# Another order for the seven products of a fused attention and MoE kernel, and for all its steps

## The chip, the cores and the metric

One core of a Trainium2 chip runs the whole program. The metric is the device time of one execution in microseconds (us); lower is better. The core has five engines with a queue each: TensorE (PE in the profile; PEld is its weight load), VectorE (DVE), ScalarE (ACT), GpSimd (POOL) and SyncE (SP), which here only issues DMA transfers.

## The reference, cut to what matters

Attention for 4 batches, 8 heads, 768 positions, 64 channels: each query sees the keys within 16 positions of it, and for each block of 32 positions one summary (the largest key channel by channel, the mean value):

```python
scores_l = scale * np.matmul(q, k.transpose(0, 1, 3, 2))      # masked to |i - j| < 16
scores_s = scale * np.einsum('bhsd,bhnd->bhsn', q, k_sum) + np.log(block)
a = softmax(np.concatenate([scores_l, scores_s], axis=-1))
x = np.matmul(a, np.concatenate([v, v_sum], axis=2))          # to 3072 rows of 512
h = x @ w_in                                                  # 512 -> 2048
return (h - np.tanh(h)) @ w_out                               # 2048 -> 512
```

## The kernel before, in words

The 3072 rows are eight units u of 384 rows (three tiles of 128). For each unit, attention runs in two halves of four heads (`block`): 48 small score products, row minimum (DVE), exponential (ACT), normalization, transposes ("p turn"), 12 value products into a bank, and a copy to SBUF. The MoE runs over 16 slices f of 128 columns of w_in: a first product into a PSUM bank of tag "pH" (two of them), an elementwise chain, a split of its result into a high and a low float32r part ("g high", "g low"), and a second product ("out", three tasks of three matmuls of 512 columns) into the banks pY0 to pY2.

A float32 product is made of three float32r products, so each matrix is kept as a high and a low part. The 32 weight slices are loaded as raw words and converted on DVE, ACT and POOL (`convert`), one after the other through the first 140 us.

From unit 2 on two units are paired, and the first product is a product of 2 by 2 blocks made of seven products instead of eight (`moe_in_seven`, L994): B11, B21, T2, T1, T3, T4 and B22, six matmuls of 384 columns each. Their left operands are slices of w_in and sums of them that `make_sums` wrote to a DRAM tensor (scr) around 80 to 235 us; `load_sums` reads them back in four loads t = 0 to 3 for each of the eight g of a pair (products 0 and 1 need t = 0, products 2 and 3 t = 1, 4 and 5 t = 2, product 6 t = 3). These loads take turns in three buffers of the tag "wraw", so the load t = 1 of the next g may start when this g's products 4 and 5 are done. Each g has two banks, z and y. Products 0, 2, 4 and 6 add up in z, 1, 3 and 5 in y (3 starts y anew); a "part" copies z to SBUF (ACT or DVE) and a "join" adds a stored part to y (DVE).

The order of the work is written out. The kernel first lists 3628 tasks with what each reads and writes; `ORDER` is a permutation of their numbers, and each engine gets its tasks in that order. `ON` has a letter for each task: which engine takes it where several could. `FILL` names tasks of PE ahead of which so many idle matmuls (two records of 128 columns each) are put, to keep PE at work through a wait. `Plan.follow` (L148) walks the list. A task waits by semaphore for what it reads and for the buffer that it writes; an engine's queue is in order, so a task that waits holds up all behind it. A helper records every instruction, so all of them carry line 56 in the profile, and are told apart by tiles.

The tile names needed here: raw weights land in wraw, their converted form in tmp and then wf; the q, k, v of the first batch land in wg, gt, gu, gv and vw; qT, kT, oo are transposed q and k; prob, probT and stat belong to the softmax; the loads of vw for a half of a unit ("v load" of 16 to 80 rows of 1 KB, 11 for each half of a unit) and three "mean put" must all have landed before the value products.

Of the kernel before, what the change touches and what calls it, by code (L numbers as in the profile page):

```python
# [21 lines left out]
RAWB = 3  # L22
# [61 lines left out]
class Plan:  # L89
# [20 lines left out]
    def add(self, kind, costs, go, r=(), w=()):  # L110
# [15 lines left out]
        for base in dict.fromkeys(key[0] for key in (*r, *w)):  # L126
# [15 lines left out]
            self.touch.setdefault(base, []).append(t)  # L142
        t.after.discard(t)
        t.order.discard(t)
        t.order -= t.after
        return t

    def follow(self, idle):  # L148

        tasks = [self.tasks[n] for n in ORDER]  # L150
        free = dict.fromkeys((PE, DVE, ACT, POOL, SP), 0.65)
        dma, held, left = 0.0, {DVE: 0.0, POOL: 0.0}, 0.0
        clock, used, seen, done = Clock(), {}, {}, []
        spot, rest, lanes = 0, self.fill, [0.0] * 8
        for t in tasks:
            e = next(iter(t.costs)) if len(t.costs) == 1 else {"D": DVE, "A": ACT, "P": POOL, "S": SP}[ON[t.index]]
            assert all(a in seen for a in (*t.after, *t.order)), t.name
            t.engine, t.cost = e, t.costs[e]
            now = max([free[e]] + [seen[a] for a in t.after] + [at for b in t.banks for a, at in used.get(b, {}).items() if a != e])
            if e == PE:  # L160
                cost, go = idle
                if now > free[PE]:
                    free[PE] = max(free[PE], min(now, seen.get(self.tasks[0], now)))
                if spot == 1:
                    free[PE] = max([free[PE]] + [min(now, at) for a, at in used.get(rest[3], {}).items() if a != PE])
                for _ in range(FILL.get(t.index, 0) if FILL is not None else int(0.7 * (now - free[PE]) / cost) if spot < 2 and now - free[PE] > 0.4 else 0):
# [171 lines left out]
def program(  # L338
# [652 lines left out]
    def gu(u, f):  # L991
        return (lambda: at(("gu", u, f))), [(("gu", u, f), 0)]
# [348 lines left out]
```

## Time and profile before

| | |
|---|---|
| time, median of 3 runs | 660.22 us (660.14 to 660.5) |
| the profiled execution: its time | 663.1 us |
| its span, first to last instruction | 661.4 us |
| mean granted TensorE clock | 0.995 |
| PE / PEld / DVE / ACT / POOL busy | 632.8 / 532.5 / 447.7 / 453.3 / 151.2 us |
| HBM read and written | 88.87 and 20.97 MB |

The page has the busy time of each engine, the span in 40 slices, the DMA queues, the chain of work that ended last, and groups of instructions. Further views give the same for a stretch of the span, the idle time of an engine by what ended it (waits), and the instructions in order of time (timeline). Matmuls overlap in the pipeline, so a row's duration is longer than the step from one matmul to the next.

### The profile page before, as it was taken

What the parts mean: (1) busy time and instruction counts of PE and PEld (TensorE: products, weight loads), DVE (VectorE), ACT (ScalarE), POOL (GpSimd) and SP (SyncE); (2) the same over time, 40 slices, a digit from 0 to 9 for tenths busy, and PEclk for the clock granted to TensorE, in tenths of its full rate; (3) what the DMA queues carried; (4) which work ended last, traced back from release to release, by engine and by line L of the source; (5) the groups of instructions that cost most, each with busy time, mean ns of one, the idle gap of its engine ahead of it and who ended that gap; (6) DMA issues with size and microseconds to landing.
All of it is one profiled execution on the core that took longest, in us unless ns stands there. A gap on an engine that the chain in (4) does not pass through costs nothing.

```text
span 661.4 us, 15115 instructions
## 1 busy us (share of the span) xinstructions
PE 632.8 (96%) x5297; PEld 532.5 (81%) x5297; DVE 447.7 (68%) x1285; ACT 453.3 (69%) x1371; POOL 151.2 (23%) x240
## 2 busy tenths in 40 slices
PE   5779989999899999999999999999999999999997
PEld 4746557778779888989888789989888799999885
DVE  2778999996998884655778874455766944334472
ACT  3578899989798863545689873644789853433773
POOL 2002310103301410113524421313343211112101
PEclk9899999999999999999999999999999999999999
DMA  7678887746687686667453465655443155444001
GB/s 201 158 212 241 230 238 223 240 146 188 209 282 259 210 266 174 194 211 219 135 156 82 115 184 178 207 163 175 136 130 84 59 173 191 146 166 153 33 17 66
DMA packets 120736, 113.24 MB, mean 171 GB/s; under 512 B 45008, under 2 KB 88528, under 8 KB 120656
## 3 DMA queue, kind: packets, MB, share of 16 engines
q1 hardware_dynamic: 117216, 109.19, 54.3%
q10 hardware_dynamic: 3440, 3.05, 1.4%
q8 instruction: 43, 0.70, 0.5%
q14 instruction: 37, 0.30, 0.2%
HBM read 88.87 MB, written 20.97 MB: 166 GB/s over the span
## 4 chain that ended last, share of the span: by engine, by line
PE 72%; DMA 12%; DVE 6%; ACT 4%; SPq 3%; issue 2%; DVEq 0%; ACTq 0%
PE pY L56 34%; PE pH L56 31%; PE pS L56 4%; DMA wraw<-in_moe_w_in_dram 3%; PE pX L56 3%; DMA raw<-in_k_dram 3%; SPq L56 3%; ACT prob L56 2%; DMA raw<-in_q_dram 1%; DMA scr<-wraw 1%; DMA wraw<-in_moe_w_out_dram 1%; DVE tmp L56 1%; DVE prob L56 1%; DVE kT L56 1%; DVE wraw L56 1%
## 5 line engine op out<-in xcount | busy, mean ns | idle before, releaser
L56 ACT ACTIVATE prob<-prob,stat 128x120 f32<-128x120 f32 x294 | 107.8, 386 | 35.4 <-DVE stat L56 34.8
L56 PE MATMUL pY<-wl,gh 128*128 128x512 f32 x288 | 113.4, 394 | 0.2 <-DVE wl L56 0.2
L56 PE MATMUL pH<-wf,wraw 128*128 128x384 f32 x552 | 112.1, 338 | 1.3 <-ACT gu L56 1.2
L56 PEld LDWEIGHTS pH<-wf,wraw 128*128 128x128 f32 x552 | 97.4, 188 | 7.1 <-ACT gu L56 1.6
L56 PE MATMUL pH<-wg,wraw 128*128 128x384 f32 x432 | 84.0, 337 | 0.2
L56 PE MATMUL pY<-wh,gh 128*128 128x512 f32 x204 | 83.2, 408 | 0.0
L56 PE MATMUL pY<-wh,gl 128*128 128x512 f32 x204 | 80.7, 396 | 0.0
L56 PEld LDWEIGHTS pH<-wg,wraw 128*128 128x128 f32 x432 | 75.9, 188 | 3.8 <-DMA wraw<-scr 0.5
L56 PE MATMUL pY<-wg,gh 128*128 128x512 f32 x168 | 68.6, 408 | 0.0
L56 ACT ACTIVATE gu<-gu 128x384 f32<-128x384 f32 x128 | 65.8, 520 | 1.9
L56 PE MATMUL pY<-wg,gl 128*128 128x512 f32 x168 | 66.5, 396 | 0.4 <-DVE gl L56 0.4
L56 PE MATMUL pH<-o,wf 128*128 128x384 f32 x188 | 65.5, 445 | 0.0
L56 POOL TENSOR_TENSOR gl<-gu,gh 128x384 fp32r<-128x384 f32 x28 | 29.5, 1055 | 144.3 <-ACT gh L56 64.1
L56 PEld LDWEIGHTS pY<-wl,gh 128*128 128x128 f32 x288 | 54.2, 188 | 9.1 <-DVE wl L56 0.6
L56 ACT ACTIVATE gv<-pH 128x384 f32<-128x384 f32 x37 | 18.1, 489 | 45.3 <-PE pH L56 45.1
L56 PEld LDWEIGHTS pH<-o,wf 128*128 128x128 f32 x188 | 34.9, 191 | 14.8 <-issue 0.9
L56 PEld LDWEIGHTS pY<-wh,gl 128*128 128x128 f32 x204 | 38.2, 187 | 8.9 <-DVE gl L56 0.4
L56 PE MATMUL pY<-wf,gh 128*128 128x512 f32 x108 | 44.5, 439 | 0.0
L56 PEld LDWEIGHTS pY<-wh,gh 128*128 128x128 f32 x204 | 38.3, 188 | 7.0 <-issue 0.5
L56 POOL TENSOR_TENSOR gu<-gu,gt 128x384 f32<-128x384 f32 x25 | 25.7, 1030 | 79.8 <-ACT gu L56 69.9
L56 ACT ACTIVATE gt<-gu 128x384 f32<-128x384 f32 x48 | 24.9, 519 | 26.9 <-DVE gu L56 25.9
L56 POOL TENSOR_TENSOR prob<-prob,stat 128x120 f32<-128x120 f32 x45 | 18.5, 415 | 89.3 <-DVE stat L56 80.3
(210 smaller groups left out, 1382.5 us busy)
## 6 DMA issues: line engine op xcount, KB each, us to landing
wraw<-scr SPq DMA_DIRECT2D x72, 512.0 KB
wraw<-in_moe_w_in_dram SPq DMA_DIRECT2D x16, 512.0 KB
wraw<-in_moe_w_out_dram SPq DMA_DIRECT2D x16, 512.0 KB
scr<-wraw SPq DMA_DIRECT2D x16, 512.0 KB
wraw<-scr SPq DMA_DIRECT2D x24, 256.0 KB
raw<-in_q_dram SPq DMA_DIRECT2D x54, 96.0 KB
vw<-in_v_dram SPq DMA_DIRECT2D x60, 80.0 KB
raw<-in_k_dram SPq DMA_DIRECT2D x48, 96.0 KB
```

The costliest lines, as they stand in the source:

```text
L56: return lambda *args, **kwargs: self._tc.keep_in_program_order(op(*args, **kwargs))
```

## The change

Four things are edited; the computation stays as it was.

1. `moe_in_seven`: the products run in the order B11, B21, T2, T1, T3, B22, T4. The part s3 is now taken from y after T1, the join c22 from z after T3, the join c12 from y after B22, and the part c21 from z comes last. In the last pair of units, the odd g use the banks pX and pS1 in place of two of tag pH.
2. The transfers "v load" of batch 0 and "mean put" of units 0 and 1 may go to POOL's DMA queue; `ON` sends ten there (v loads 8, 13, 20, 23, 26, 38, 40; mean puts 0, 2, 5). Before, SP issued all of them.
3. `ORDER`, `ON` and `FILL` are new throughout.
4. Buffers wl, vw, qT and kT are taken from another pool; a DRAM tensor scr2 and functions for a second seven-product scheme are added (`make_out_sums`, `moe_out_seven`), which nothing calls, since `OUT7` is empty.

```diff
-FILL = {125: 18, 154: 12, 158: 2, 190: 14, 188: 6, 286: 2}
+FILL = {125: 16, 154: 12, 158: 2, 190: 10, 188: 1, 215: 2, 262: 2, 286: 2}
+OUT7 = ()
-    def dma(kind, go, nbytes, run, r=(), w=(), both=False):
+    def dma(kind, go, nbytes, run, r=(), w=(), both=False, any_queue=False):
...
+        elif small_only and any_queue:
+            t = plan.add(kind, {SP: cost, POOL: cost}, go, r, w)
...
-        z, y = bank(("z", u, g), "pH"), bank(("yx", u, g), "pH")
+        tags = ("pX", "pS1") if u == NU - 2 and g % 2 else ("pH", "pH")
+        z, y = (bank((n, u, g), tag) for n, tag in zip(("z", "yx"), tags))
...
         product(0, "B11", z, True)
         product(1, "B21", y, True)
-        part(lambda: at(s1), [(s1, 0)])
-        join(c11, k11, s1)
+        part(z, lambda: at(s1), [(s1, 0)])
+        join(y, c11, k11, s1)
         product(2, "T2", z, False)
-        part(lambda: at(s2), [(s2, 0)])
+        part(z, lambda: at(s2), [(s2, 0)])
         product(3, "T1", y, True)
+        part(y, lambda: at(s3), [(s3, 0)])
         product(4, "T3", z, False)
-        part(lambda: at(s3), [(s3, 0)])
-        join(c22, k22, s3)
+        join(z, c22, k22, s3)
+        product(5, "B22", y, False)
+        join(y, c12, k12, s2)
         load_sums(u, g, 3)
         product(6, "T4", z, False)
-        part(c21, k21)
-        product(5, "B22", y, False)
-        join(c12, k12, s2)
+        part(z, c21, k21)
```

What the new lists say, with tasks of the two lists matched by name:

| KB of transfers issued, up to and with | before | after |
|---|---|---|
| weight load 0 | 3696 | 3632 |
| k loads 8 to 11 (second half of heads) | 4400 | 4080 |
| weight load 1 | 5296 | 5152 |
| all of vw for unit 0, heads 0 to 3 | 5792 | 5792 |
| all of vw for unit 0, heads 4 to 7 | 8000 | 7488 |
| weight load 3 | 7152 | 7376 |
| weight load 4 | 7808 | 8336 |
| q loads 8 to 11 (unit 1) | 8464 | 8480 |
| weight load 9 | 11584 | 11712 |

On PE the first 160 us hold the same tasks at places that differ by a few. On DVE the transpose of k loads 8 to 11 now stands ahead of the last step of weight 0 and of the next six minima, that of k loads 12 to 15 behind four of these; one normalization that stood ahead of them, the scaling of weights 2 and 3, and the means 5 and 6 of the first value sums went to ACT. On POOL, mean put 2 and six further transfers stand behind two normalizations of the first softmax. Ahead of the score products of unit 3, heads 4 to 7 (the seventh block), the copy "top put 3" went from ACT to DVE, and the first product of unit 1, slice 5, which stood directly ahead of them, is now followed by a value and an out task. The 16 guards of softmax sums moved from DVE to POOL are spread over the whole run. Products of PE between the products 4 and 5 of a g, whichever comes last, and product 2 of the next g: before 4.0 to 7.1 us at the durations of the trace, in 15 of 21 cases under 4.3; after 4.5 to 9.3. The tail behind the last product is as before, but for the queue of two stores.

## Rows read from the trace of the kernel before

**Rows 1.** Windows by stage: length, busy time of each engine (instructions), PE clock, DMA share, GB/s
```profile
0.00:16.50 16.50, 8.77 (x122) 8.11 (x125) 4.66 (x5) 5.20 (x20) 4.43 (x28) 1.00 0.76 201
16.50:33.00 16.50, 12.52 (x274) 11.54 (x266) 11.53 (x43) 8.83 (x36) 0.63 (x2) 0.90 0.63 159
...
100.00:150.00 50.00, 50.00 (x491) 36.31 (x486) 48.69 (x134) 46.38 (x135) 4.57 (x5) 1.00 0.69 203
...
550.00:600.00 50.00, 50.00 (x265) 46.66 (x264) 20.24 (x39) 19.58 (x49) 4.15 (x5) 1.00 0.47 159
```

**Rows 2.** Waits of PE over the span: total us, times, longest
```profile
PE pH L56 <- DMA gt<-in_v_dram: 6.7, 2, 4.0
PE pS L56 <- DVE prob L56: 4.6, 2, 4.0
PE pY L56 <- ACT tmp L56: 3.2, 1, 3.2
PE pH L56 <- ACT gt L56: 2.7, 1, 2.7
...
PE pH L56 <- ACT gu L56: 1.2, 1, 1.2
```

**Rows 3.** Timeline of PE, 18 to 50 us: start, length, what, [idle before]
```profile
18.34 2.94 PE L56 MATMUL pY<-ident 128*128 128x128 f32 x24
25.27 0.89 PE L56 MATMUL pS<-ident,prob 128*120 128x128 f32 x4 [3.98 <-DVE prob L56]
...
27.11 4.54 PE L56 MATMUL pY<-ident 128*128 128x128 f32 x28
...
35.51 0.45 PE L56 MATMUL pS<-probT,vw 120*64 120x64 f32 x8 [0.33 <-DMA vw<-in_v_dram]
...
46.02 0.95 PE L56 MATMUL pY<-probT,wg 120*64 120x64 f32 x24 [3.21 <-ACT tmp L56]
```

**Rows 4.** Timeline of DVE, 20 to 33 us
```profile
22.97 0.43 DVE L56 TENSOR_SCALAR tmp<-wraw 128x512 f32<-128x512 f32 x1 [2.26 <-DMA wraw<-in_moe_w_in_dram]
...
25.13 0.88 DVE L56 SCALAR_TENSOR_TENSOR wf<-wraw,tmp 128x512 uint32<-128x512 uint32 x1
25.93 0.27 DVE L56 CUSTOM_DVE_ANT_0 prob<-pX,mask 128x120 f32<-128x120 f32 x1
...
27.67 1.83 DVE L56 STREAM_TRANSPOSE wg<-wg 128x768 f32<-128x768 f32 x2
```

**Rows 5.** Timeline of SP's DMA issues, 0 to 60 us
```profile
16.71 1.00 SPq L56 DMA_DIRECT2D vw<-mean  x1
17.77 0.47 SPq L56 DMA_DIRECT2D wraw<-in_moe_w_in_dram  x1
...
26.86 6.06 SPq L56 DMA_DIRECT2D vw<-in_v_dram  x5
```

**Rows 6.** Waits of SP's queue, 0 to 60 us
```profile
SPq L56 <- DMA raw<-in_q_dram: 3.8, 1, 3.8
```

**Rows 7.** Windows of 4 us, columns as in Rows 1
```profile
16.00:20.00 4.00, 3.98 (x154) 3.73 (x155) 2.01 (x8) 0.48 (x2) 0.00 (x0) 1.00 0.42 105
...
32.00:36.00 4.00, 3.67 (x121) 2.79 (x117) 3.53 (x18) 3.67 (x14) 0.25 (x1) 1.00 0.51 142
...
48.00:52.00 4.00, 4.00 (x33) 2.35 (x32) 2.72 (x6) 1.94 (x5) 0.00 (x0) 0.72 0.93 267
```

**Rows 8.** Timeline of POOL, 10 to 60 us
```profile
25.08 0.39 POOL L56 TENSOR_TENSOR prob<-prob,stat 128x120 f32<-128x120 f32 x1 [10.16 <-DVE stat L56]
```

**Rows 9.** Timeline of ACT, 163 to 172 us
```profile
167.59 0.53 ACT L56 ACTIVATE kT<-kT 128x384 f32<-128x384 f32 x1 [2.46 <-DVE kT L56]
```

**Rows 10.** Timeline of SP's DMA issues, 232 to 262 us
```profile
253.91 4.29 SPq L56 DMA_DIRECT2D wraw<-scr  x3
```

**Rows 11.** Timeline of PE, 258 to 260 us
```profile
259.73 0.59 PE L56 MATMUL pH<-wf,wraw 128*128 128x384 f32 x2 [1.19 <-ACT gu L56]
```

**Rows 12.** Chain that ended last, pieces in order of time: start, length
```profile
227.85 4.28 DMA wraw<-scr
```

**Rows 13.** Timeline of PE, 540 to 552 us
```profile
548.10 2.25 PE L56 MATMUL pH<-wg,wraw 128*128 128x384 f32 x12
```

More of the change, by code (lines that the diff above doesn't have):

```diff
@@ L177, in follow @@
                 now = max(now, free[PE])
-                if t.kind in ("in", "out", "p turn"):
+                if t.kind in ("in", "out", "out half", "p turn"):
                     t.cost, left = t.cost + max(left, 0.0), -1.0
@@ L181, in follow @@
                     t.cost, left = t.cost + (self.ENTERS if left < 0 else 0.0), self.LEAVES.get(t.kind, 0.0)
+            elif SP in t.costs and e == POOL:
+                now = max(now, others.pop(0), held[DVE])
+                t.issue, t.ahead, held[POOL] = 0.62, 1.8, now + 0.62
             elif SP in t.costs:
@@ L672, in program @@
         made[SCR] = spool.tile([FH, 8, P, 2 * DH], F32, name="scr")
+        made[SCR2] = spool.tile([5, FH, P, 2 * DH], F32, name="scr2")
     def make_sums(g):
@@ L1017, in product, with part, join @@
             do("in", PE, 1.055, go, r=[(st, 0)] + [key for c in range(2) for _, key in x_of[x, u, c]], w=[(ps, 0)])
-        def part(out, keys):
-            either("part", {ACT: 0.4, DVE: 0.49}, lambda e: copy(e, out(), at(z)[:, :U]), r=[(z, 0)], w=keys)
-        def join(out, keys, x):
-            do("join", DVE, 0.47, lambda: vector.tensor_tensor(out(), at(y)[:, :U], at(x), op=ALU.add), r=[(y, 0), (x, 0)], w=keys)
+        def part(ps, out, keys):
+            either("part", {ACT: 0.4, DVE: 0.49}, lambda e: copy(e, out(), at(ps)[:, :U]), r=[(ps, 0)], w=keys)
+        def join(ps, out, keys, x):
+            do("join", DVE, 0.47, lambda: vector.tensor_tensor(out(), at(ps)[:, :U], at(x), op=ALU.add), r=[(ps, 0), (x, 0)], w=keys)
         for t in range(3):
@@ L1274, in program @@
                 convert(2 * m2[1] + 1)
-            moe_out(*m2)
-            if m2[1] == order_of(m2[0])[-1]:
+            if not seven_out(m2[0]):
+                moe_out(*m2)
+            if not seven_out(m2[0]) and m2[1] == order_of(m2[0])[-1]:
                 for i in range(NT):
@@ L1289, in program @@
                 moe_in_seven(*m)
-            moe_act(*m)
+                if seven_out(m[0]):
+                    for n in range(4):
+                        moe_act(m[0] + n % 2, m[1] + FH * (n // 2))
+            if not seven_out(m[0]):
+                moe_act(*m)
             if small_only and m[0] == 1 and 5 <= m[1] < FH + 5:
                 make_sums(m[1] - 5)
-        if m1 is not None and not (m1[0] == 0 and m1[1] in WHOLE_F):
+            if small_only and OUT7 and j >= 36 and (j - 36) % 3 == 0 and (j - 36) // 3 < FH:
+                make_out_sums((j - 36) // 3)
+        if m1 is not None and not (m1[0] == 0 and m1[1] in WHOLE_F) and not seven_out(m1[0]):
             moe_split(*m1)
```

173 lines of the change are left out of this document (157 added, 16 removed).

## The prediction

> **What bounds the kernel now.** I read the windows by stage first, then the waits of PE, then the timelines of the stretches in which PE waits. In the windows the reader is to see three phases [rows 1]. To 33 us PE has work for 8.77 + 12.52 of 33 us, and part of that is idle matmuls. DVE and ACT are not full either, and the DMA engines are busy 0.76 and then 0.63 of the time: the stretch waits for transfers. From 100 to 150 us PE is busy for all of 50 us with DVE at 48.69 and ACT at 46.38 us, so an earlier start there must be paid by three engines. From 550 to 600 us PE is full and DVE and ACT stand at 40%: only fewer or shorter matmuls would help there, and the change has the same ones.
>
> The waits say what can be won [rows 2]: 13.9 us in three causes before 50 us (DMA gt 6.7, DVE prob 4.0 of its 4.6, ACT tmp 3.2), and 2.7 and 1.2 us in single waits later; the rest is small. So the reorder of the seven products by itself stands where PE never waits. The place to look at is the start.
>
> In the start the chain reads thus. PE's first transposes begin at 25.27 after 3.98 us of idleness that follow 12 idle matmuls [rows 3]. They wait for DVE, which itself waited 2.26 us for the first weight until 22.97 [rows 4]. That load was issued at 17.77, behind a mean put that held SP's queue from 16.71 [rows 5]. Meanwhile the DMA engines idled: 0.42 busy and 105 GB/s from 16 to 20 us, 0.51 and 142 from 32 to 36 [rows 7]. In the second gap SP stood 3.8 us for an earlier q load to land [rows 6], inside the 6.06 us row of five v loads [rows 5]. After that PE lacks the value products at 46.02, 3.21 us late [rows 3]. The named ACT row is a weight scaling on which they don't depend; the tile wg that they read gets its last v loads shortly before, so I take it for a DMA. After the idleness the granted clock falls, to a mean of 0.72 in 48 to 52 us [rows 7], so part of that stretch ran at 1.2 GHz.
>
> **The change part by part**, against the profiled execution (663.1 us, span 661.4; 2.9 us above the median of 660.22, so I carry the difference over to the median).
>
> *Start, first weight.* 64 KB fewer are issued ahead of weight 0, and SP no longer issues mean put 2 (1.00) and v load 13 (about 0.4) there. Weight 0 is issued some 1.4 us earlier; the bound is 0 to the 2.26 us that DVE waited [rows 4]. I take 1.5, as the mean put's row lies directly ahead of the load's row [rows 5]. The first transposes start 1.5 us earlier.
>
> *Start, second half of the heads.* The score products behind 28 idle records (14 of FILL, 4.54 us, [rows 3]) need k loads 8 to 15, their transposes and the maxima on DVE. 320 KB fewer stand ahead of k loads 8 to 11, 1.6 us at the 201 GB/s of the first window [rows 1]. The first transpose (half of the 1.83 us row at 27.67) runs before the 0.88 us step of weight 0 and the minima [rows 4], so it fills a time in which DVE waits today; DVE has otherwise the same work ahead of the maxima. The ten fillers that remain cost 10/14 of 4.54 = 3.2 us, so these scores can gain at most 1.3 us over the transposes. I take 0.5 more, 2.0 in all (0 to 2.8).
>
> *Start, value products.* For heads 0 to 3 the KB ahead are equal (5792), so they gain only what better filled DMA gaps give. For heads 4 to 7 it is 512 KB less, 2.6 us at 201 GB/s, against the 3.21 us wait. DVE's chain there sheds its wait for weight 3, which ACT scales now, but weight 3 has 224 KB more ahead of it (1.1 us), and ACT's next normalizations queue behind it. Ends: 0 and 3.2 on top of the earlier gain, and no more than about 4.5 with it; I take 3.0 in all by 46 us. With less idleness the stretch at half clock may shrink: a mean of 0.72 over 4 us costs 1.1 us [rows 7]; I take 0.5, between 0 and 1.1. Sum at 50 us: 3.5 us earlier.
>
> *The ten transfers on POOL.* No row shows a transfer issued there. From below I take SP's 0.4 (v load) and 1.00 (mean put, [rows 5]), from above 1.4, three to four times POOL's 0.39 us normalization [rows 8]. POOL idles 10.16 us ahead of that row, so its time costs nothing; what counts is when mean put 0 lands, the sixth transfer behind the two normalizations. They end at about 25.9 less 1.5, and six issues at 0.8 bring it to 29.2; five v loads took SP until 32.92 [rows 5], and the products went on at 35.51, 2.6 us later [rows 3]. So it lands at about 32, in time. This costs 0; if each issue took 1.4 us it would be 32.8 + 2.6 = 35.4, no gain for these products and no loss.
>
> *What survives to 150 us.* KB ahead of q loads 8 to 11 (8464 and 8480) and of weight 9 (11584 and 11712) are equal, so beyond 55 us an earlier start holds only if the DMA gaps [rows 7] are filled; and DVE idles 1.31 of 50 us after 100 us [rows 1]. It moves forward with the rest, but its work does not shrink. I give back 1.5 of 3.5: 2.0 stay (0 to 4.5).
>
> *Seventh block's scores, at 171 us.* PE waits 2.7 us for ACT there [rows 2], and ACT had itself waited 2.46 us for DVE's kT ahead of the copy at 167.59 [rows 9]. The copy goes to DVE, so ACT does its next seven instructions while DVE finishes kT. The bank is then free earlier, but the scores still need kT and its copy, at about 168. I take 1.2 (0 to 2.7).
>
> *Seven products.* Two products take 2.25 us [rows 13], so 168 products are the same work in either order. What differs is the buffer: the load t = 1 of the next g starts when products 4 and 5 are done, and a load of scr took 4.28 us [rows 12]. Before, PE has 4.0 to 4.3 us of other work in 15 of 21 cases; after, 4.5 to 9.3. In one case the cover failed: SP's three loads span 253.91 to 258.20 [rows 10], and product 2 began at 259.73 after 1.19 us of idleness [rows 11]. The row names ACT; the load fits better. This goes: 1.2 (0 to 1.2). The copies hide behind a product of about 1.1 us [rows 13]; in four places only two out tasks stand between product 6 and product 0 of the next g, which needs the same bank, and an ACT or DVE that is late shows there. I charge 1.5 us for such new waits over the whole run (0 to 4), since each wait of [rows 2] after 60 us came from an engine that was late in the same way. The banks pX and pS1 take this dependence away in the last pair. Fillers: 54 before, 47 after, counted above.
>
> Sum: -2.0 - 1.2 - 1.2 + 1.5 = -2.9 us: 660.2 for a profiled execution, 657.3 us by the median.
>
> **The rivals.**
>
> *A, nothing is won at the start.* The stretch is bound by bytes, not by issue: the equal KB ahead of weight 9 speak for it, the two gaps of [rows 7] against it. Then only 1.2 + 1.2 - 1.5 are left: 659.3 us, within the noise.
>
> *B, POOL's transfers come late (slower).* Place: the first value products, which need mean put 0, the sixth in line. If each waited for the DVE instruction under way, 1 us in the mean with the 1.83 us row among them [rows 4], an issue would cost 1.8 us and the last come at 24.4 + 10.8 = 35.2, landing at 37.8 against 35.51 - 0.4 us now: 2.7 us late instead of 3.5 early. Then +2.7 - 1.2 - 1.2 + 1.5 = +1.8: 662.0 us. It decides from a start of these products after about 38 us. POOL's idleness [rows 8] speaks against it; that no row shows such a transfer leaves it open.
> The Trainium skill (SBUF — State Buffer, section "SBUF: two separate sides") states a rule that would bring this about: a transfer issued from GpSimd's queue has its descriptors made by GpSimd's cores, which cannot write them while VectorE holds the shared port in a two-port operation. By that rule DVE, busy for 11.53 of 16.5 us there, makes these transfers late, and B's time follows; no run here shows it yet.
>
> *C, the whole front is kept.* DVE and DMA follow, and the new waits stay away: -3.5 - 1.2 - 1.2 = -5.9, 654.3 us. The full DVE of 100 to 150 us speaks against it.
>
> *D, the reorder itself counts.* Since PE is full without waits around 550 us, it can give only the 1.2 us above; that is in the sum.
>
> **How the numbers follow.** The measurement cannot tell less than 0.2% (1.3 us) from no change. Forecast (655.7 to 658.9): 0.50. A: 0.22, a third of it below 658.9. B: 0.13. C: 0.15. Faster: 0.50 + 0.15 + 0.07 = 0.72; same 0.15; slower 0.13. The likeliest case gives 657.3. The range from 653.9 to 661.0 holds the forecast, A and most of C, and leaves out B's 662.0 and the end of C.
>
> **What would show it.** Right: DMA busy well above 0.42 around 16 to 20 us and no 3.8 us wait of SP; the first transposes before 24.3 us; the second half's value products before 44; no clock loss around 50 us; PE's wait at the seventh block under 1.7 us; no wait of over 0.3 us at a product 2. Wrong: value products of heads 0 to 3 after 36 us (B); an early start that is gone by 100 us, with waits of PE for weights between 80 and 100 us (A); or new waits of more than 2 us between 230 and 530 us, at the last part of z.

## The result and the profile after

The changed kernel takes 652.81 us (median of 19 runs) beside 660.98 us for the kernel before (19 runs): a ratio of 0.9887, 95% interval 0.9868 to 0.9907. Measured again in a later comparison it took 653.18 us, 0.9885 (0.9846 to 0.9924). The gain is 7.4 to 8.2 us; forecast were 2.9, with 653.9 as the lower end of the range. The profiled execution took 653.67 us, its span 651.8.

The windows by stage, columns as in [rows 1], and three of 4 us, which answer to [rows 7]:

```profile
0.00:16.50 16.50, 10.08 (x170) 9.01 (x177) 5.28 (x6) 4.72 (x20) 4.60 (x25) 1.00 0.90 231
16.50:33.00 16.50, 12.99 (x252) 11.60 (x240) 12.03 (x55) 11.46 (x46) 6.18 (x15) 0.90 0.73 176
100.00:150.00 50.00, 49.09 (x488) 36.52 (x488) 46.66 (x131) 44.57 (x133) 6.96 (x9) 1.00 0.71 215
550.00:600.00 50.00, 50.00 (x261) 46.36 (x260) 17.61 (x35) 20.63 (x54) 9.32 (x9) 1.00 0.49 164
16.00:20.00 4.00, 1.71 (x96) 1.43 (x96) 2.95 (x16) 3.01 (x15) 1.29 (x7) 1.00 0.79 182
32.00:36.00 4.00, 3.31 (x57) 2.65 (x57) 3.90 (x20) 4.00 (x17) 0.00 (x0) 1.00 0.87 222
48.00:52.00 4.00, 4.00 (x13) 2.12 (x12) 4.00 (x18) 2.17 (x9) 0.00 (x0) 1.00 0.73 217
```

The DMA gaps of 0.42 and 0.51 are filled (0.79, 0.87), and 48 to 52 us runs at full clock. PE's waits, which answer to [rows 2]:

```profile
PE pH L58 <- POOL ident L58: 4.1, 1, 4.1
PE pS L58 <- ACT prob L58: 2.5, 2, 1.3
PE pX L58 <- issue: 2.3, 1, 2.3
PE pH L58 <- DMA gu<-in_v_dram: 1.7, 2, 1.0
PE pH L58 <- DVE qT L58: 1.3, 1, 1.3
...
PE pH L58 <- DMA gt<-in_v_dram: 0.6, 1, 0.6
...
PE pH L58 <- DMA wraw<-scr: 0.2, 1, 0.2
```

The 4.0 us for DVE (of the 4.6) and the 3.2 us of before are gone. The 6.7 us are not, though the prediction counts them among what can be won: 4.0 of them stand ahead of PE's first instruction, and the changed kernel has this wait under another name (4.1, POOL ident); of the other 2.7, 2.3 are still there (gt and gu). PE's timelines of before and of the changed kernel:

```profile
3.98 0.39 PE L56 MATMUL pH<-gt,wh 128*32 128x64 f32 x2 [3.98 <-DMA gt<-in_v_dram]
```

```profile
4.14 0.39 PE L58 MATMUL pH<-gt,wh 128*32 128x64 f32 x2 [4.14 <-POOL ident L58]
```

PE's timeline answers to [rows 3]: the first transposes begin at 24.51 (25.27), the value products of heads 0 to 3 at 31.87, and all in one row (before, the last of them were held up until 35.51), those of heads 4 to 7 at 40.14 (46.02). What stands ahead of the first transposes is no longer DVE but 24 idle records, 4.57 us long (the granted clock is 0.58 from 20 to 24 us):

```profile
20.10 4.57 PE L58 MATMUL pY<-ident 128*128 128x128 f32 x24
24.51 0.60 PE L58 MATMUL pS<-ident,prob 128*120 128x128 f32 x4
...
31.87 0.92 PE L58 MATMUL pS<-probT,vw 120*64 120x64 f32 x24
...
40.14 0.92 PE L58 MATMUL pY<-probT,wg 120*64 120x64 f32 x24
```

**One profile is not the kernel.** Before was profiled once more (its expectation stands below): 660.34 us, where the first profile had 663.1. Of the rows that the prediction rests on, the lowered clock of 48 to 52 us (0.72) and the stall of 1.19 us at 259.73 [rows 7, 11] are not in it (1.00 from 48 to 52, PE busy all 12 us from 250 to 262), and the value products of heads 4 to 7 start at 43.34, behind a wait that names a v load, as the prediction had read the one at 46.02; the wait at the seventh block is there (2.43). Windows of the second profile of before:

```profile
48.00:52.00 4.00, 4.00 (x107) 2.98 (x106) 2.75 (x6) 2.85 (x9) 0.00 (x0) 1.00 0.91 243
250.00:262.00 12.00, 12.00 (x154) 11.13 (x153) 6.07 (x27) 6.27 (x22) 0.00 (x0) 1.00 0.60 185
```

And its timeline of PE:

```profile
23.68 0.89 PE L56 MATMUL pS<-ident,prob 128*120 128x128 f32 x4 [2.13 <-DVE prob L56]
...
43.34 0.93 PE L56 MATMUL pY<-probT,wg 120*64 120x64 f32 x24 [1.27 <-DMA wh<-in_v_dram]
...
169.64 0.28 PE L56 MATMUL pH<-kT,qT 32*64 32x120 f32 x1 [2.43 <-ACT gt L56]
```

The changed kernel has a second profile too (after_again, 653.1 us). In it the 24 idle records take 2.94 us, with a granted clock of 1.00 from 20 to 24 us, and the transposes and both groups of value products come 1.3 to 2.7 us earlier than in the first. PE's timeline:

```profile
19.02 2.94 PE L58 MATMUL pY<-ident 128*128 128x128 f32 x24
21.80 0.60 PE L58 MATMUL pS<-ident,prob 128*120 128x128 f32 x4
...
30.40 0.92 PE L58 MATMUL pS<-probT,vw 120*64 120x64 f32 x24
...
38.82 0.92 PE L58 MATMUL pY<-probT,wg 120*64 120x64 f32 x24
```

To compare kernels whose tasks stand in another order I counted, from each trace, the PE work done by a time t (each task at its median length, idle matmuls not counted) and took the difference to this second profile of before, in us:

```
t                   25   40   50   60   80  120  170  200  230  300  400  600
first profile     -0.3 -0.8 -3.7 -3.7 -1.1 -1.5 -0.4 -0.9 -1.1 -2.5 -2.5 -2.7
changed           -0.2  2.0  2.9  2.9  3.8  2.9  2.9  4.4  3.8  4.5  5.6  6.1
changed, again     0.5  3.2  2.9  2.9  3.4  3.3  3.3  4.6  4.0  4.7  6.0  6.5
front_after        0.5  2.4  3.3  2.3  3.3  3.5  2.6  3.4  2.5  2.6  3.0  3.0
front_before       0.1  1.4 -1.1 -0.9 -0.3 -0.9 -0.0  0.9 -0.2  0.5  0.8  0.7
paired_before      0.6  3.2  2.7  2.6  2.1  2.1  3.1  4.8  2.3  1.2  1.7  1.7
paired_after      -0.2  0.5 -3.7 -4.0 -2.1 -2.6 -0.7 -1.3 -0.9 -1.2 -1.1 -0.7
no_pool_queue     -0.0 -0.4 -0.6 -1.3 -1.8 -2.2 -1.1 -0.9 -2.9 -2.5 -1.0 -1.1
before_pool        0.3  2.3 -0.2  0.3  1.7  1.9  0.8  2.2  1.7  1.5  2.2  2.1
before_pool_early  0.1  1.8  2.3  3.0  2.2  2.0  0.4  0.2  0.2 -0.0  0.6  0.9
means_on_pool     -0.0  2.6  2.5  1.6  0.7  1.7  1.9  3.8  2.7  3.4  4.5  5.0
more_pool          0.6 -1.1 -2.5 -2.3 -0.6 -0.4  0.5  2.2  1.0  1.5  2.6  3.0
engines_before    -0.3 -0.1 -0.6 -3.7 -2.2 -2.8 -1.2 -1.1 -2.4 -1.6 -0.5 -0.3
split_loads        0.0  2.2  1.3  0.8  0.3  0.5  0.9  2.9  1.3  2.0  2.7  3.1
split_late         0.4  3.8  3.2  3.5  1.3  2.4  2.8  4.1  3.5  4.2  5.1  5.5
split_late_2       0.0  2.3  3.2  3.8  4.5  3.3  1.6  2.8  1.2  1.9  3.2  3.6
swap_two           0.5 -0.0  0.3  0.9  0.1 -0.2  0.4  1.7  0.6  1.3  2.3  2.7
fewer_fill         0.5  2.8  3.0  3.2  2.4 -0.1  1.1  2.9  1.2  0.3  1.5  1.6
```

So the changed kernel wins 2.9 us before 50 us and keeps them, 1.3 to 1.5 between 170 and 200, and 2.3 to 2.5 between 230 and 600, where PE's waits come to 0.6 us in this profile of before and to 0.4 in the changed kernel. Each row is one execution, and executions of one kernel spread by 3 to 9 us, so medians decide the sizes and the table shows only where. The early columns also hang on how the work is weighed: with each matmul at the median step of its shape, the changed kernel's two profiles are 1.6 to 1.9 us ahead at 50 and 60 us and 3.4 to 3.9 at 170; from 200 us on the two counts agree to 0.3. Behind 230 us the rows form two groups: the thirteen traces with the new list there win 0.2 to 2.5 us from 230 to 600 (median 2.0), the six with the list of before, its second profile among them, -1.6 to 0.7 (median 0.2).

### The profile page after: what moved, and what is told of

It reads as the page before. It is cut to its first block, busy times and chain, and to the rows that moved or that the text cites. A ratio compares the mean times of both kernels' runs of the same rounds, so it can differ in the third digit from the quotient of the medians.

```text
span 651.8 us, 15139 instructions
## 1 busy us (share of the span) xinstructions
PE 629.3 (97%) x5283; PEld 532.4 (82%) x5283; DVE 446.8 (69%) x1271; ACT 451.8 (69%) x1372; POOL 163.8 (25%) x263
## 4 chain that ended last, share of the span: by engine, by line
PE 77%; DMA 7%; DVE 7%; ACT 5%; issue 2%; SPq 1%; POOL 0%; DVEq 0%; ACTq 0%
PE pY L58 38%; PE pH L58 28%; PE pS L58 6%; PE pX L58 5%; ACT prob L58 3%; DVE tmp L58 2%; DMA wraw<-in_moe_w_in_dram 2%; SPq L58 1%; DVE wf L58 1%; DMA raw<-in_q_dram 1%; DMA raw<-in_k_dram 1%; DMA wraw<-scr 1%; DMA gu<-in_v_dram 1%; DMA wraw<-in_moe_w_out_dram 1%; DVE prob L58 1%
## 5 line engine op out<-in xcount | busy, mean ns | idle before, releaser
L58 ACT ACTIVATE prob<-prob,stat 128x120 f32<-128x120 f32 x299 | 109.5, 389 | 14.6 <-DVE stat L58 14.4
L58 PE MATMUL pH<-wf,wraw 128*128 128x384 f32 x460 | 93.7, 339 | 0.3 <-DVE wf L58 0.2
L58 PEld LDWEIGHTS pH<-wf,wraw 128*128 128x128 f32 x460 | 80.9, 188 | 3.6 <-DVE wf L58 0.5
L58 PE MATMUL pH<-wg,wraw 128*128 128x384 f32 x360 | 71.0, 338 | 0.0
L58 POOL TENSOR_TENSOR gl<-gu,gh 128x384 fp32r<-128x384 f32 x32 | 34.1, 1066 | 129.2 <-ACT gh L58 77.4
L58 PEld LDWEIGHTS pH<-wg,wraw 128*128 128x128 f32 x360 | 63.4, 188 | 3.1 <-issue 0.8
L58 POOL TENSOR_TENSOR gu<-gu,gt 128x384 f32<-128x384 f32 x26 | 27.2, 1048 | 75.4 <-ACT gu L58 68.1
L58 PEld LDWEIGHTS pY<-wg,gl 128*128 128x128 f32 x168 | 31.5, 188 | 7.3 <-DVE gl L58 0.4
```

## The experiments

The medians of before in the four comparisons of several runs are 660.6 to 661.4 us. Where the ratios to before put a kernel at another distance from the changed one (0.9887) than the medians do, both distances are given. The two lists have nearly the same tasks in their first 250 and first 1470 places, so they can be joined there (PE is then at 45 us and at 231 us in the changed kernel). Every kernel here except before itself is built from the changed kernel's code, with the buffers of its fourth edit, and no run has that edit alone. front_before and paired_after have it and stand at 1.000 and 0.998, so it does not carry the gain by itself; in before_pool and before_pool_early it is a part of what is measured.

### Which stretch wins

```diff
 front_before:  ORDER[:250], with ON and FILL of these tasks: before; rest: changed
 front_after:   ORDER[:250]: changed, eight of the ten transfers on POOL; rest: before, old products
 paired_after:  ORDER[:1470]: before; rest: changed
 paired_before: ORDER[:1470]: changed; rest: before, old products
```

> The changed kernel, but its first 250 tasks (to about 45 us of PE's time) are in the order, on the engines and with the idle matmuls of the kernel before; the rest is as changed. Theory (the front's gain is kept to the end): the trace of the changed kernel has done 7.1 us more of PE's work by 55 us and 4.7 us more by 230 us, so this kernel loses 4 to 5 us against the changed one: 657 us, a ratio to before of about 0.994. Rival 1 (the front is given back, as in the prediction: 2.0 us survive): 654.8 us, 0.991. Rival 2 (the stretch from 65 to 150 us is bound by DVE and ACT, the front counts nothing): 652.8 us, 0.988.

Measured: 660.21 us, 1.000 (0.9971 to 1.0029). All of the gain goes, more than either side expected.

> The reverse: the first 250 tasks as in the changed kernel, with its ten transfers on POOL, and the rest as before, with the old order of the seven products. Theory (the front is kept): 4 to 5 us faster than before, 656.5 us, ratio 0.993. Rival 1 (2.0 us survive): 659 us, 0.997. Rival 2 (the front counts nothing): 661 us, 1.000.

Measured: 655.32 us, 0.9917 (0.9885 to 0.9949): 3.4 to 7.6 us faster. By its median the front alone carries 5.7 of the 8 us, and it is kept. Its expectation speaks of ten transfers on POOL; two of them lie behind the 250 tasks and are SP's in this kernel.

> Everything to about 231 us as before (the first 1470 tasks), the rest as changed, with the new order of the seven products everywhere. Theory (half of the gain comes behind 230 us, where the work done by the changed kernel goes from 4.9 to 9.4 us ahead): 4.5 us faster than before, 656.5 us, ratio 0.993. Rival (as predicted, only the one stall near 259 us goes and new waits cost as much): 660 to 661 us, 0.999 to 1.000.

Measured: 660.44 us, 0.9982 (0.9952 to 1.0012). The rival stands: the paired part gives at most 3.2 us without the front.

> The changed kernel to about 231 us (its first 1470 tasks), the rest as before, with the old order of the seven products everywhere. Theory (from the traces so far: behind 230 us the changed kernel wins 4.5 us against the one profiled run of before, but before's own lists win 2.6 of these in the kernel with the changed front; 1.9 us belong to the change): 654.7 us, ratio 0.990 to 0.991. Rival 1 (all 4.5 us belong to the paired part): 657 us. Rival 2 (none): 652.8 us.

Measured: 654.79 us, 0.9896 (0.9877 to 0.9914), five runs, 1.6 to 2.0 us above the two measurements of the changed kernel by the medians and 0.6 by the ratios. That is the time of the theory, but the intervals of the two kernels overlap, so the times alone do not rule out rival 2. In its row of the table nothing is won from 230 us on (2.3 to 1.7).

### The order of the seven products alone

```diff
 ORDER, ON, FILL: before
-B11 B21 T2 T1 T3 T4 B22
+B11 B21 T2 T1 T3 B22 T4   (each product, part and join in a place of its block)
```

> The kernel before with the new order of the seven products alone (each product, part and join takes a place that its block already had; transfers, engines, idle matmuls and the rest of the list as before). Theory (as predicted, this alone can give the one stall near 259 us and costs as much in new waits): 660 to 661 us, ratio 0.998 to 1.000. Rival (the new order makes PE's work itself shorter or frees buffers in all 24 blocks): 658.5 us or less, ratio under 0.9965.

Measured: 700.20 us, 1.057 (1.0544 to 1.0597). Both were wrong. PE's timeline shows how it goes from block to block, some 39 us over 24 blocks:

```profile
275.69 1.49 PE L58 MATMUL pH<-wf,wraw 128*128 128x384 f32 x6 [2.05 <-DVE gv L58]
276.98 0.63 PE L58 MATMUL pY<-wh,gh 128*128 128x512 f32 x1
277.40 0.63 PE L58 MATMUL pY<-wf,gh 128*128 128x512 f32 x1
...
290.37 1.32 PE L58 MATMUL pH<-wf,wraw 128*128 128x384 f32 x6 [1.03 <-DVE gv L58]
```

A block now ends with a product in z, the bank that the next block's first product needs. In the old list nothing stands between the two: PE waits for the reading of it (gv, by DVE in these rows), and after the longer wait the granted clock falls (0.58 in the mean of 276 to 280 us; output products start 0.43 us apart, where 0.23 is usual). In the changed list other steps stand there, and no such wait is on its page. The product order and the list are one edit. The new list with the old order was not tried.

### The queue of the ten transfers

```diff
 no_pool_queue:     changed; ON of the ten transfers 'P' -> 'S'
 before_pool:       before; the ten transfers on POOL, at their old places
 before_pool_early: before; the ten on POOL, at their places in the changed list
 means_on_pool:     changed; v loads of the ten 'P' -> 'S', mean puts stay
 more_pool:         changed; v loads 6, 10, 11, 21, 22, 24 'S' -> 'P'
```

> The changed kernel with its ten transfers issued by SP again, at the same places of the list. Theory (SP's queue is what the front waited for): SP gets 7 v loads of about 0.45 and 3 mean puts of about 0.85 to 1.0 us back, some 6 us of issue inside the first 60 us, so the value products come 2 to 3 us later and the time is 1.5 to 2.5 us above the changed kernel: 654.3 to 655.3 us. Rival (the order alone makes the front, the second queue is spare): within 0.7 us of the changed kernel, 652.1 to 653.5 us.

Measured: 657.98 us, 0.996 (0.9937 to 0.9982), 5 us above the changed kernel, twice what the theory said. In the profiled execution, the slowest of the twelve, SP issues one transfer behind the other from 20.34 to 47.24 us, and from 28 to 36 us of that the DMA engines are at 0.39 and 0.43 of their time (0.81 and more from 36 to 48 us). Windows:

```profile
28.00:32.00 4.00, 2.85 (x104) 2.14 (x102) 3.36 (x17) 3.53 (x15) 0.00 (x0) 1.00 0.39 89
32.00:36.00 4.00, 1.55 (x24) 1.39 (x24) 0.91 (x7) 2.26 (x11) 0.00 (x0) 0.65 0.43 110
```

The value products wait for a mean put (33.97 for 31.87; those of heads 4 to 7 start at 44.13 for 40.14). PE's timeline:

```profile
33.97 1.55 PE L58 MATMUL pS<-probT,vw 120*64 120x64 f32 x24 [2.53 <-DMA vw<-mean]
```

And SP's, with the last mean put of that half:

```profile
30.75 1.73 SPq L58 DMA_DIRECT2D vw<-mean  x1
```

From 28 to 36 us this kernel is short of issues, not of bytes. The Trainium skill (Perfetto Trace Analysis, section "DMA Optimizations") says that balancing transfers over the engines that can issue them may help where descriptor generation is the limit; the row of 0.39 agrees.

> The kernel before, with the one edit that the ten transfers are issued by POOL, at their places in the old list. Theory (issue slots: what the front waits for is SP's queue, one issue after another at 0.45 to 1.0 us, whatever the list): SP is freed of some 6 us as in the changed kernel, the value products of heads 0 to 3 and 4 to 7 come 2 to 4 us earlier, and the time falls by 3 to 5 us to 656 to 658 us, ratio 0.992 to 0.995. Rival (queue and order need each other: in the old list the ten stand behind POOL's normalizations and SP waits for buffers, not for slots): at most 1 us, 660 to 661 us, ratio 0.998 to 1.000.

Measured: 658.98 us, 0.9961 (0.9932 to 0.9989): half of the theory. POOL's queue, which is in order, held three of the transfers behind a normalization. POOL's timeline:

```profile
35.37 0.64 POOL L58 TENSOR_TENSOR prob<-prob,stat 128x120 f32<-128x120 f32 x1 [4.48 <-DVE stat L58]
36.02 0.63 POOL L58 DMA_DIRECT2D wg<-mean  x1
36.69 0.67 POOL L58 DMA_DIRECT2D wg<-in_v_dram  x1
37.34 0.58 POOL L58 DMA_DIRECT2D vw<-in_v_dram  x1
```

Heads 4 to 7 waited for v loads until 42.10. PE's timeline:

```profile
42.10 1.55 PE L58 MATMUL pY<-probT,wg 120*64 120x64 f32 x24 [2.41 <-DMA wg<-in_v_dram]
```

> The kernel before, with the ten transfers on POOL and moved to the places that they have in the changed list; all else as before. With POOL at the old places the time was 2.4 us below before (0.9961). Theory (places: there POOL's in-order queue issued four of them at 35 to 38 us only, behind normalizations): 3.5 to 5 us below before, ratio 0.992 to 0.9945. Rival (the rest of the front's order is what is missing): again about 2.4 us, 0.995 to 0.9965.

Measured: 658.48 us, 0.9957 (0.9929 to 0.9984). The wait is gone (heads 4 to 7 at 40.58) and its trace is 3.0 us ahead at 60 us, yet 0.4 at 170, and the time is that of before_pool: the rival stands. The queue alone brings some 2 us. What it wins by 60 us is lost again in this execution; in that of front_after, which has the order and the engines of the front too, it is not (2.3 us at 60, 2.6 at 170).

> The changed kernel with only the three mean puts on POOL and the seven v loads back on SP. Theory (issue slots, in proportion): the three mean puts take 0.83 to 1.0 us each of SP, 2.7 us, the five v loads of the front about 0.45 each, 2.3 us; so somewhat under half of the 5.2 us comes back: 654.5 to 655.5 us. Rival 1 (what decides is that the mean puts, on which all value products wait, go past SP's queue): within 0.7 us, 652.1 to 653.5 us. Rival 2 (the v loads decide): 657 to 658 us.

Measured: 657.29 us, 0.9935 (0.9908 to 0.9962), near rival 2. But its profiled execution has nearly the gain of the changed kernel (5.0 us at 600); which transfers decide is open.

> The changed kernel with six more v loads of unit 0 on POOL (three for heads 0 to 3, three for heads 4 to 7), sixteen transfers in all. Theory (behind 32 us the front is bound by DVE and ACT, which are busy for 3.5 to 4.0 of every 4 us there; SP's slots no longer decide): within 0.7 us of the changed kernel, 652.1 to 653.5 us. Rival 1 (slots still decide): 1 to 2 us faster, 651 to 652 us. Rival 2 (POOL's queue, in which a mean put waits for ACT until 27.4 us, holds up what stands behind it): 1 to 3 us slower, 654 to 656 us.

Measured: 657.22 us, 0.9946 (0.9922 to 0.997). Rival 2, by another way: behind the fifth of them in a row POOL's queue itself stops, five times, for 1.1 to 2.1 us, with no releaser that the profile shows. POOL's timeline:

```profile
29.03 0.60 POOL L58 DMA_DIRECT2D vw<-mean  x1
31.73 0.61 POOL L58 DMA_DIRECT2D wg<-in_v_dram  x1 [2.11 <-issue]
```

The mean puts take 5.6 us from issue to landing, where the changed kernel has 2.5, in its second profile 3.2 (the page's DMA issues: count, KB each, median us):

```profile
vw<-mean POOLq DMA_DIRECT2D x2, 48.0 KB, 5.6
```

And PE waits 6 us for one:

```profile
35.52 1.55 PE L58 MATMUL pS<-probT,vw 120*64 120x64 f32 x24 [6.07 <-DMA vw<-mean]
```

Such a stop does not need sixteen transfers. In the second profile of the changed kernel the queue stops once, ahead of the eighth; in front_after, with eight in all, it stops there for 2.20 us. POOL's timeline in the second profile of the changed kernel:

```profile
27.33 0.68 POOL L58 DMA_DIRECT2D wg<-in_v_dram  x1 [1.31 <-issue]
```

### Issues or bytes, and how much a disturbance costs

```diff
 split_loads: changed; v loads 5, 6, 7, 9, 10, 11, 12, 21, 22, 24 as two halves each
 split_late:  changed; v loads 52, 62 to 69, 77 (about 95 to 130 us) as two halves each
 swap_two:    changed; v loads 5 and 6 exchanged
```

> The changed kernel with ten of the v loads that SP issues for unit 0 (seven for heads 0 to 3, three for heads 4 to 7) each issued as two transfers of half the rows: the same bytes, ten more issues on SP, POOL's queue as changed. Theory (issue slots: the front waits for SP's queue at 0.4 to 0.5 us for each issue, not for bytes): 4.5 us more of issue before about 40 us, so about as bad as all ten back on SP, 3 to 5 us above the changed kernel: 656 to 658 us. Rival (bytes, or something that only POOL's queue brings): within 0.7 us, 652.1 to 653.5 us.

Measured: 656.23 us, 0.9924 (0.9896 to 0.9953), 2.4 to 3.4 us above. By bytes this should have cost nothing; its trace loses 1.6 to 2.1 us by 60 us.

> The changed kernel with ten v loads of the stretch of about 95 to 130 us issued as two halves each: the same ten more issues on SP as in the split loads of the front, but where SP is thought to wait for buffers, so that it has spare slots. Theory (slots decide in the front alone): within 0.7 us of the changed kernel beside it. Rival 1 (any disturbance): 655.5 to 658 us. Rival 2 (SP has no spare slots there either, and weights come later): 1 to 3 us slower.

Measured: 657.62 us, 0.9952 (0.9917 to 0.9986). The theory is wrong here: the control costs as much as the split in the front, so split_loads does not show that issues are what its ten halves cost. Its runs spread from 652.8 to 661.7 us, and its profiled execution (654.42) shows no loss. A second profile, for a slow execution:

> The kernel with ten v loads of about 95 to 130 us split once more, for a second profile. Theory (the split loads make late weights in some executions): if this execution is above 656 us, PE waits for weights between 80 and 140 us and part of that stretch runs at the lower clock; if below, no wait differs from the changed kernel by over 0.5 us. Rival (the time is lost elsewhere, at the start or behind 230 us).

It took 656.31 us and was level with the changed kernel at 120 us (3.3 us ahead); by 170 us it had fallen 1.3 behind, in a stretch where PE waits 1.0 and 0.4 us for the softmax and 1.3, as the changed kernel, for the transpose of q. No weight is waited for: the theory's cause is not shown, the place lies half in it; open.

> The changed kernel with two neighbouring transfers of SP exchanged in the front (the v loads 5 and 6, 80 KB each, both needed by the same value products): a disturbance that adds no issue, no byte and no wait. Theory (issue slots): within 0.7 us of the changed kernel beside it. Rival (any disturbance of this list costs 3 to 5 us): 655.5 to 658 us.

Measured: 654.37 us, 0.9896 (0.9861 to 0.9931). It cannot be told from the changed kernel, so not every disturbance costs 3 to 5 us.

> The changed kernel once more, as it is, beside the next three. Theory (the edits so far cost what they measured): 652 to 653.5 us, ratio 0.987 to 0.991. Rival (the first measurement of it was a lucky one): 655 us or more, ratio 0.992 or more, and the losses of the edits shrink by as much.

Measured: 653.18 us, 0.9885: the first measurement was no luck.

> The kernel before once more, for a second profile. Theory (the paired part's gain of 4.5 us over the first profile was partly that execution's own: two kernels that keep before's lists behind 231 us did 2.6 and 1.5 us better there): the stall of 1.2 us near 259 us is absent or smaller, and PE's work in 231 to 660 us is 1.5 to 2.6 us ahead of the first profile. Rival (the stall belongs to the list): the same stall, within 0.5 us.

Measured: 660.34 us, one execution; the stall is absent and 1.4 us are won from 230 to 300 us, as expected.

### Engines and idle matmuls of the front

```diff
 engines_before: changed; ON of 41 steps among the first 250 as before
 fewer_fill:     changed
-FILL = {125: 16, 154: 12, ...
+FILL = {125: 16, 154: 2, ...
```

> The changed kernel with the 41 steps among its first 250 tasks that changed their engine back on the engine that they had before (26 steps of DVE, ACT and POOL, among them the scalings of weights 2 and 3, the means 5 and 6 and a copy of half of kT; and k and q loads between SP's and ACT's queue); order, idle matmuls and the ten transfers on POOL as changed. Theory (the other half of the front's gain is the order and these engines together; DVE and ACT are both full behind 32 us): 1 to 3 us above the changed kernel, 654 to 656 us. Rival (the engines decide nothing): within 0.7 us, 652.1 to 653.5 us.

Measured: 657.96 us, 0.9934 (0.9908 to 0.996): 3 to 5 us above the changed kernel. The engines are as much a part of the front as the queue: from 48 to 52 us PE is busy for 1.83 of 4 us.

> The changed kernel with 2 instead of 12 idle matmuls (4 records for 24) ahead of the first transposes of the softmax. In the changed kernel these 24 records take 4.57 us at half clock, to 24.67 us, while POOL has the first two normalized tiles at 21.8 us, and DVE then waits 1.99 us until 25.04 for the transposes to free its buffers. Theory (they hold up the front): first transposes at about 22 us, DVE's minima 2 us earlier, time 1 to 2 us below the changed kernel: 651 to 652 us. Rival 1 (the value products wait for their transfers at about 31.5 us anyway): within 0.5 us, 652.3 to 653.3 us. Rival 2 (the clock, now 0.58 in 20 to 24 us, stays at half for longer without them): 1 to 2 us slower, 654 to 655 us.

Measured: 657.07 us, 0.993 (0.9904 to 0.9956), 3 to 4 us above. The transposes did begin at 20.87, but the granted clock was 0.50 from 20 to 24 us and 0.75 from 24 to 28 (0.58 and 0.99 in the first profile of the changed kernel), as rival 2 had it. By 50 us the front ran no earlier (3.0 for 2.9), so the 24 records held up nothing. What the theory had not seen came at 105 us; from 80 to 120 us the trace loses 2.5 us (2.4 to -0.1): ACT waits 2.2 us for a weight to land, PE 1.9 us for its conversion, and then the clock is at 0.66. Windows:

```profile
105.00:110.00 5.00, 3.66 (x14) 2.26 (x12) 2.88 (x6) 3.70 (x10) 0.00 (x0) 1.00 0.62 176
110.00:115.00 5.00, 4.47 (x13) 2.08 (x13) 5.00 (x10) 3.65 (x9) 1.16 (x1) 0.66 0.83 248
```

Why that weight was late is not settled. No version beat the changed kernel.

## Why the prediction was wrong

*Start, first weight: mis-sized, no harm.* Weight 0 is issued 4.7 us earlier, not 1.4 (at 13.01 and 12.67 in the two profiles, 17.77 and 17.40 before), and DVE takes it without a wait. It is no longer what the transposes wait for. They begin at 24.51, behind idle matmuls at the lowered clock, or at 21.80: 0.8 us later or 1.9 earlier than in the second profile of before (23.68), where 1.5 were taken.

*Start, second half and value products: right.* 3.5 us by 50 us were forecast; it is 2.9 against the second profile of before (6.6 against the first, whose lowered clock and late value products were its own). PE comes to the next block of score products (kT, qT) at 45.97 and 44.65 us in the two profiles of the changed kernel, at 49.16 in that of before. But I worked in KB ahead. What no_pool_queue shows is SP's issues: 10 transfers off its queue, with 33.97 for 31.87 as the price of not doing it.

*The ten transfers on POOL at no cost: right.* An issue took 0.60 to 0.81 us (taken: 0.8), and the value products came at 31.87 and 30.40. Rival B did not come about, though DVE was busy for 12.03 of 16.5 us. The rule of the Trainium skill (SBUF — State Buffer, section "SBUF: two separate sides") is about VectorE's two-port operations, and the busy time does not tell how much of it they are, so it gave no ground to take all of the prediction's 11.53 us. The queue did stop, for 1.31 us in the second profile and longer in more_pool; whether for this cause no run shows.

*What survives: wrong, the step that failed.* I gave back 1.5 of 3.5 because DVE was full from 100 to 150 us and the KB ahead of weight 9 equal. Nothing was given back: 2.9 us at 60 us, 2.9 to 3.3 at 170. By front_after the front is worth 3.4 to 7.6 us, not 2.0. DVE's work was moved too: 48.69 us of it in 100 to 150 became 46.66 (47.52 in the second profile). That is not what kept the gain: front_after has the list of before there, and DVE about as full, and is still 3.5 us ahead at 120 us. Why a full DVE took nothing back stays open. Window of front_after:

```profile
100.00:150.00 50.00, 49.54 (x489) 36.72 (x489) 47.78 (x138) 45.48 (x136) 5.43 (x6) 1.00 0.67 200
```

*Seventh block: right in size, wrong in cause.* The wait fell from 2.43 to 1.31 us (1.61 in the second profile). The copy of kT that moved to DVE ended at 161.62, 4.4 us ahead of the scores, which wait for the transpose of q; the copy decides nothing now. DVE's timeline, then PE's:

```profile
161.23 0.39 DVE L58 COPY kT<-kT 128x384 f32<-128x384 f32 x1
```

```profile
166.01 0.28 PE L58 MATMUL pH<-kT,qT 32*64 32x120 f32 x1 [1.31 <-DVE qT L58]
```

*Seven products: wrong, with the sign.* The 1.2 us of the stall belonged to one execution. The 1.5 us for new waits did not come (longest at a product: 0.2), and the stretch won 2.3 to 2.5 us by the table, 0.6 to 2.0 by paired_before, where I had a loss of 0.3. I took "PE busy for 50 of 50 us" [rows 1] for a bound. It is not: the first output product behind an attention step holds the next one until 0.31 to 0.34 us after its start, where 0.23 is usual, and that time counts as busy. PE's timeline in the second profile of before:

```profile
327.36 0.50 PE L56 MATMUL pY<-wh,gh 128*128 128x512 f32 x1
327.70 0.39 PE L56 MATMUL pY<-wl,gh 128*128 128x512 f32 x1
327.93 0.39 PE L56 MATMUL pY<-wh,gl 128*128 128x512 f32 x1
```

Behind 235 us there are 37 such places in the second profile of before and 26 in the changed kernel, 1.0 us. The rest lies in the steps between output products that follow each other directly: 231.2 ns in the mean in both profiles of before, 229.2 in both of the changed kernel, which comes to 1.5 us over some 740 of them behind 235 us. This is not the spread of executions, and it is not the order of the products: front_after and paired_before, with the list of before behind 231 us, have 229.5 and 229.4; front_before and paired_after, with the new list there and the old front, have 231.0 and 230.9. The shorter step comes with the first 250 tasks; by what, stays open.

Of the 4.5 to 5.3 us between forecast and result, the table thus puts 2.6 to 2.8 behind 230 us and 0.9 to 1.3 in what survives of the front; by the median of front_after the front, which brings the shorter steps too, has the larger share. Rival C (654.3) was the nearest. D, that the order of the products could give 1.2 us by itself, is refuted: alone it costs 39 us.

## What to carry to other kernels

Where many transfers of 16 to 80 KB start a kernel, count issues for each queue, at the row's 0.4 to 1.0 us, before counting bytes; a queue issuing without a break beside idle DMA engines is the sign. A list of steps, its engines and its queues are tuned together: setting back the front lost all of the gain, the queue or the engines 3 to 5 us of it, and the product order moved alone cost 39. And profile both kernels twice before resting a term on a single wait: 1.7 us of this forecast's terms were one execution's.

## What was not expected of the hardware

POOL's queue took ten transfers with 0.60 to 0.81 us for an issue and 2.5 to 4.6 us to landing, and stopped once, for 1.31 us, in one of two profiles; with six more it stopped five times for 1.1 to 2.1 us between issues. Behind 235 us the mean step between output products depends on the order of the first 250 tasks (229.1 to 229.5 ns in the 13 traces with the new one, 230.8 to 231.2 in the 7 with the old one). The same kernel with ten loads split ran between 652.8 and 661.7 us on one chip.
